# Hashed attention and channel mix on one core: pairs 2 and 3 prepared by the joint q-and-k path, with a new hand-off order for all engines

## The chip, the cores and the metric

The kernel runs on one core of a Trainium2 chip. A core has five engines that each work through their own list of instructions in order: TensorE (PE in the profile, its weight loads PEld), VectorE (DVE), ScalarE (ACT), GpSimd (POOL) and SyncE (SP, which here only starts DMA transfers). They wait for one another through semaphores. The metric is the device time of one execution in microseconds; lower is better.

## What is computed

Inputs are q, k and v of shape (4, 8, 768, 64), a projection of 64 by 6, and the weights of a channel mix. For each of the 32 (batch, head) pairs the reference computes

```python
q_bucket = np.sum(((q @ proj) > 0) * powers, axis=-1)      # six sign bits per row
k_bucket = np.sum(((k @ proj) > 0) * powers, axis=-1)
scores = np.where(q_bucket[..., :, None] == k_bucket[..., None, :], (q @ k.T) / 8, -1e9)
attn = softmax(scores)                                      # over the keys
x = (attn @ v)                                              # heads put side by side: (4, 768, 512)
xk = mu_k * x + (1 - mu_k) * x_prev                         # x_prev: one row earlier
xr = mu_r * x + (1 - mu_r) * x_prev
out = sigmoid(xr @ w_r) * (relu(xk @ w_k) ** 2 @ w_v)
```

The output is (4, 768, 512) in float32.

## The kernel before

**Pairs.** The work on attention is cut into 16 pairs n = 0 to 15. A pair is two heads of one batch (j = 0, 1), and four pairs make up a batch. After the fourth pair of a batch its channel mix (`add_moe`) can run.

**The steps of a pair.** For pair n the names are these. `ldq` (L330) brings q and k of both heads into `nat`, `ldv` (L335) brings v into `vn`. `hi` (L398, DVE) rounds q and k to float16 into the first 64 columns of `nh`, and `lo` (L401, DVE) writes the rounding remainder into the other 64. `tr` (L405, SP) is a DMA that transposes `nh` into `a`, where the rows are the head dimension and the columns the sequence. `bits` (L427, PE) projects `a` to the hash bits; `bx` (L431, DVE) turns the signs into +-64 values; four `row` copies (L443, POOL), one for each of q0, q1, k0 and k1, put them into six rows of `a`, so that one matmul gives the score and the bucket comparison together. `sc` (L544, PE) makes nine tiles of scores (`scn_0` to `scn_8`, 1024 columns each), `exp` (L548, ACT) turns each into probabilities. `oo` (L566 and L571, PE) multiplies with v, `rc` and `ob` (DVE) divide by the row sum, `ot` (PE) or `otd` (SP, a transposing DMA) transposes the result, and `xt`, `xs`, `df`, `xk`, `xr` (DVE) mix it with the row before. `vsum` (L356 to L362, POOL) and `mean` (PE) prepare v.

**Three ways of preparing.** Pairs 0 and 1 (`FIRSTS`) are transposed on PE without any DMA (`add_prep_turn`: `y`, `x`, `t` on PE at L478, L489 and L512, `ey` and `ev` on ACT or DVE, `ex` on DVE at L497). All other pairs go through `add_prep`. A pair that isn't in `MERGED` runs `hi`, `lo` and `tr` twice, once for q and once for k, each over half of the buffers; a pair in `MERGED` runs each once over the whole buffer. In both cases q and k of a pair lie in the two halves of the same buffers, `nat` (three of them), `nh` (two) and `a` (four).

```python
whole = n in MERGED
for side in ("qk",) if whole else "qk":
    nat, nh, a = (nat_t[s], nh_t[sh], a_t[sa]) if whole else (side_nat[side][s], ...)
```

**Channel mix.** `kp` (L659, PE), `relu` (ACT), `sq` (DVE), `r` (L679, PE), `tanh` (ACT), `v` (L692, PE), `os` (L699, DVE) and `st` (L702, SP: the store). Its weights come in by `wl` (SP) and are cast by `wc` (POOL).

**The order.** The functions only describe operations, in program order. The list `ORDER` (L17) gives the sequence in which all of them are issued, as indices into that program order; it was computed ahead of time and is written out. Because every engine works in order, `ORDER` fixes each engine's own sequence. `BANKS` (L72) gives each PSUM tile, in program order, its place: 0 to 3 for a 4 KB score tile, 0 to 7 for a half of one. A tile can be written only after the last reader of the tile that had the place before. `warm` and `warmb` (L246, L251) are matmuls on zeros that keep PE occupied; `warm` is 14 of them, each of the eight `warmb` is two. `table` (L253, ACT) makes ACT load its function table.

Of the kernel before, what the change touches and what calls it, by code (L numbers as in the profile page):

```python
# [128 lines left out]
def kernel(  # L129
# [34 lines left out]
    MERGED = tuple(range(4, 16))  # L164
# [225 lines left out]
    def add_prep(n):  # L390
        s, sh, sa = n % NQ, n % NNH, n % NAQ
        whole = n in MERGED
        for side in ("qk",) if whole else "qk":
# [385 lines left out]
```

## Time and profile before

| What | Value |
|---|---|
| three runs | 243.22, 243.06, 242.08 us; median 243.06 us |
| the profiled execution | 242.0 us, of which the span from first to last instruction is 240.2 us |
| granted TensorE clock, mean | 1.00 |
| busy of the span | PE 97%, DVE 75%, ACT 76%, POOL 41% |
| DMA queue q1 | 43.20 MB, 70.9% of the 16 DMA engines' span |

Busy counts the time in which at least one instruction of the engine runs. The profiled execution takes 1.8 us more than its span; that lies before the first and after the last instruction. A figure such as "x12" in a row is a count of instructions, and "idle before" names what the engine waited for.

### The profile page before, as it was taken

To read this page: it belongs to the slowest core of one execution; us is meant where nothing else is said; L and a number is where in the kernel's file an instruction comes from. 1 tells how busy PE (TensorE), PEld (TensorE's weight loads), DVE (VectorE), ACT (ScalarE), POOL (GpSimd) and SP (SyncE) were. 2 spreads that over 40 slices of the span, in tenths; PEclk is the share of its full clock that TensorE was granted. 3 is DMA by queue.
4 is the path that set the end of the run, shared out by engine and by line. 5 is a ranking of instruction groups with operands and counts; after the bars stand their busy time and mean duration, and the time that the engine had idled before them with its cause. 6 is when DMAs were issued, how large, how long until landed. Compare 5 with 4: busy or idle time off the path is not lost.

```text
span 240.2 us, 6251 instructions
## 1 busy us (share of the span) xinstructions
PE 234.1 (97%) x2515; PEld 147.8 (62%) x2532; DVE 179.8 (75%) x388; ACT 181.9 (76%) x242; POOL 99.7 (41%) x148
## 2 busy tenths in 40 slices
PE   8999999999999999999999999999999999999994
PEld 6985776776766565656456656665566564455442
DVE  3488789999998898989868896887167867348232
ACT  2699999999999999889779999677884640256320
POOL 4064979989934899438087302550000000000000
PEclk9999999999999999999999999999999999999999
DMA  6989999999999999988999989401500401210333
GB/s 225 304 222 274 232 242 260 279 197 362 279 253 284 273 213 294 249 302 206 276 163 241 249 177 234 136 0 26 173 0 3 120 3 44 87 46 1 131 135 131
DMA packets 72605, 44.00 MB, mean 183 GB/s; under 512 B 54912, under 2 KB 67584, under 8 KB 72576
## 3 DMA queue, kind: packets, MB, share of 16 engines
q1 hardware_dynamic: 72208, 43.20, 70.9%
q8 instruction: 20, 0.33, 0.6%
q10 hardware_dynamic: 368, 0.39, 0.5%
q14 instruction: 9, 0.07, 0.1%
HBM read 24.12 MB, written 6.29 MB: 127 GB/s over the span
## 4 chain that ended last, share of the span: by engine, by line
PE 92%; ACT 5%; issue 1%; DVE 0%
PE ps_all L544 25%; PE ps_all L692 17%; PE ps_all L659 16%; PE ps_all L571 14%; PE ps_all L679 8%; ACT pt L548 4%; PE ps_all L427 4%; PE ps_all L489 2%; PE ps_all L512 1%; PE ps_all L478 1%; ACT kr L663 1%; PE ps_all L251 1%; PE ps_all L246 1%; PE ps_all L599 1%; PE ps_all L566 1%
## 5 line engine op out<-in xcount | busy, mean ns | idle before, releaser
L548 ACT ACTIVATE pt<-ps_all 128x1024 bf16<-128x1024 f32 x144 | 138.4, 1041 | 10.9 <-PE ps_all L544 10.3
L544 PE MATMUL ps_all<-a 128*128 128x256 f16 (+1 forms) x384 | 79.2, 325 | 0.5 <-ACT pt L548 0.3
L443 POOL COPY a<-bx 6x384 f32<-6x384 f32 x56 | 38.9, 695 | 34.4 <-DVE bx L431 19.6
L544 PEld LDWEIGHTS <-a 128*128 128x128 f16 x384 | 34.0, 98 | 23.5 <-issue 4.6
L659 PE MATMUL ps_all<-xk,wk 128*128 128x384 bf16 x256 | 48.3, 326 | 0.1
L571 PEld LDWEIGHTS <-pt 128*128 128x128 bf16 x1152 | 42.5, 97 | 8.0 <-issue 0.5
L692 PE MATMUL ps_all<-wv,k 128*128 128x512 bf16 (+2 forms) x199 | 45.6, 362 | 0.5
L571 PE MATMUL ps_all<-va,pt 128*128 128x65 bf16 x1152 | 44.8, 193 | 0.0
L663 ACT ACTIVATE kr<-ps_all 128x384 bf16<-128x384 f32 x64 | 29.4, 491 | 16.0 <-PE ps_all L659 14.4
L659 PEld LDWEIGHTS <-wk 128*128 128x128 bf16 x256 | 24.2, 98 | 17.0 <-issue 0.6
L692 PEld LDWEIGHTS <-k 128*128 128x128 bf16 x208 | 19.3, 98 | 18.9 <-issue 0.3
L699 DVE SCALAR_TENSOR_TENSOR os<-rs,ps_all 128x512 f32<-128x512 f32 (+2 forms) x26 | 16.5, 643 | 19.0 <-PE ps_all L692 13.7
L682 ACT ACTIVATE rs<-ps_all 128x512 f32<-128x512 f32 x24 | 14.3, 602 | 20.5 <-PE ps_all L679 14.1
L666 DVE TENSOR_TENSOR k<-kr 128x384 bf16<-128x384 bf16 x64 | 23.2, 389 | 8.3 <-ACT kr L663 8.3
L401 DVE SCALAR_TENSOR_TENSOR nh<-nat,nh 128x1536 f16<-128x1536 f32 (+1 forms) x16 | 27.0, 1694 | 0.2
L679 PE MATMUL ps_all<-wr,xr 128*128 128x512 bf16 x88 | 23.2, 379 | 0.4
L356 POOL TENSOR_TENSOR vt<-vn 128x384 f32<-128x384 f32 x12 | 17.8, 1485 | 12.5 <-DMA vn<-in_v_dram 11.7
L589 DVE TENSOR_TENSOR ob<-ps_all,rc 128x384 bf16<-128x384 f32 x32 | 17.5, 553 | 1.4 <-DMA xt<-ob 0.8
L431 DVE TENSOR_SCALAR bx<-ps_all 128x768 uint16<-128x768 uint16 x14 | 13.4, 956 | 5.3 <-PE ps_all L427 4.7
L398 DVE TENSOR_SCALAR nh<-nat 128x1536 f16<-128x1536 f32 (+1 forms) x16 | 15.8, 985 | 0.3 <-PE ps_all L512 0.2
L679 PEld LDWEIGHTS <-xr 128*128 128x128 bf16 x96 | 9.0, 98 | 9.0
L380 DVE SCALAR_TENSOR_TENSOR va<-ps_all,vn 128x384 bf16<-128x384 f32 x24 | 12.7, 548 | 0.5 <-PE ps_all L375 0.2
(77 smaller groups left out, 188.9 us busy)
## 6 DMA issues: line engine op xcount, KB each, us to landing
vn<-in_v_dram SPq DMA_DIRECT2D x16, 384.0 KB, 5.1
out_dram<-os SPq DMA_DIRECT2D x23, 256.0 KB, 2.3
nat<-in_k_dram SPq DMA_DIRECT2D x15, 384.0 KB, 4.7
nat<-in_q_dram SPq DMA_DIRECT2D x15, 384.0 KB, 5.2
wst<-in_moe_w_k_dram SPq DMA_DIRECT2D x2, 512.0 KB, 7.0
wst<-in_moe_w_r_dram SPq DMA_DIRECT2D x2, 512.0 KB, 5.8
wst<-in_moe_w_v_dram SPq DMA_DIRECT2D x2, 512.0 KB, 4.4
k<-in_moe_w_k_dram SPq DMA_DIRECT2D x1, 512.0 KB, 4.4
```

Of the source, the lines that this page charges most:

```text
L356: e.tensor_tensor(out=vt[:, :, :, 0:E], in0=src[:, :, 0:3, 0:E], in1=src[:, :, 3:6, 0:E], op=ALU.add)
L401: nc.vector.scalar_tensor_tensor(out=nh[:, :, D:P], in0=nat.rearrange("p j (c d) -> p (j c) d", d=D), scalar=QS, in1=nh[:, :, 0:D], op0=AL ...
L443: nc.gpsimd.tensor_copy(side_a[side][n % NAQ][D : D + NB, j, :].bitcast(FP32), bx_t[sx][32 * i : 32 * i + NB, :].bitcast(FP32))
L544: nc.tensor.matmul(ps[:, lo - s * STEP : hi - s * STEP], side_a["k"][sa][:, j, jc * P : (jc + 1) * P], side_a["q"][sa][:, j, q0 : q0 + hi ...
L548: nc.scalar.activation(out=pt_t[sp][:, s * STEP : (s + 1) * STEP], in_=ps_t[plan.slot[nm]], func=AF.Exp, bias=EBIAS, scale=ESC)
L571: nc.tensor.matmul(oo[:, ic * 65 : ic * 65 + 65], pt_t[sp][:, o : o + P], va_t[sa][:, j, jc, 0 : D + 1], start=(not uc and ic == 0 and jc ...
L589: nc.vector.tensor_tensor(out=ob_t[so][:, :, j * D : (j + 1) * D], in0=oo[:, :, 0:D], in1=rc_t[sr][:, 1, :].unsqueeze(2).to_broadcast([P, ...
L659: nc.tensor.matmul(ps[:, 0:HALF], wk_sb[:, d, fc * P : (fc + 1) * P], xk_t[mx[d]][:, h * HALF : (h + 1) * HALF], start=(d == 0), stop=(d = ...
L663: nc.scalar.activation(out=kr_t[sk], in_=sm(nm)[:, 0:HALF], func=AF.Relu, scale=0.5 ** 0.5)
L666: nc.vector.tensor_tensor(out=k2_t[s2][:, h * HALF : (h + 1) * HALF], in0=kr_t[sk], in1=kr_t[sk], op=ALU.mult)
L679: nc.tensor.matmul(sm(nr), xr_t[mx[d]][:, c * P : (c + 1) * P], wr_sb[:, d, :], start=(d == 0), stop=(d == NDC - 1))
L692: nc.tensor.matmul(sm(nv)[:, x0:x1], k2_t[(b * NFC + fc) % NK2][:, c * P : (c + 1) * P], wv_sb[:, fc, x0:x1], start=(fc == 0), stop=(fc == ...
```

## The change

`MERGED` now begins at 2 instead of 4. Pairs 2 and 3 thereby have one `hi`, one `lo` and one `tr` each instead of two, six operations fewer in all (1326 instead of 1332), and the indices in `ORDER` shift. `ORDER` and `BANKS` are replaced throughout.

```diff
 ORDER = [
-    0, 16, 2, 3, 4, 21, 5, 6, 7, 20, 8, 9, 10, 11, 37, 41, 33, 26, 1, 29, 28, 36, 30, 32, 40, 69, 72, 71, 70, 74, 73, 25, 43, 27, 31, 79,
+    69, 0, 2, 3, 4, 5, 6, 7, 8, 9, 10, 11, 12, 16, 31, 13, 14, 15, 84, 72, 1, 39, 42, 71, 74, 25, 32, 70, 24, 33, 73, 77, 75, 76, 90, 78,
...
 BANKS = [
-    2, 6, 2, 0, 4, 0, 0, 0, 0, 4, 4, 0, 3, 7, 1, 5, 4, 6, 1, 4, 5, 3, 4, 5, 2, 3, 4, 5, 4, 3, 0, 1, 2, 3, 0, 0, 0, 1, 7, 6, 6, 0, 2, 2, 2,
+    4, 2, 7, 3, 3, 2, 3, 7, 4, 3, 0, 0, 2, 4, 7, 1, 6, 6, 5, 2, 1, 1, 4, 7, 4, 2, 0, 1, 0, 3, 2, 2, 0, 1, 0, 1, 1, 3, 0, 1, 1, 3, 2, 1, 0,
...
-    MERGED = tuple(range(4, 16))
+    MERGED = tuple(range(2, 16))
```

Read as names, engine by engine, the beginnings of the two orders are these (a digit after a name is the pair, "1k" is q or k of pair 1; `oo0_0` stands three times in the list because it is issued in three parts):

```
SP before  0q0 0q1 pw1 1k 2k mur 2q 3k 1q v0 v1 3q tr2 tr2 4k v2 4q muk v3 tr3 tr3 5q 5k tr4 6q 6k v4 tr5 wl2 v5 wl0 wl1 tr6
SP after   0q0 0q1 pw1 1k v0 1q v1 2q 2k v2 4k 3q 3k tr2 4q v3 v4 muk tr3 5q 5k mur 6k 6q tr4 v5 v6 tr5 wl0 wl1 tr6
ACT before 0k0 0k1 pw0 ey0k0 ey0q0 ey0q1 ey0k1 table evt0k0 ey1k0 evt0k1 exp0_1 ...
ACT after  0k0 0k1 table pw0 ey0q0 ey0k0 ey0k1 ey0q1 evt0k0 ey1k0 evt0k1 exp0_1 ey1q0 ...
PE before  [14 warm, warmb 0 5 4 3] y0k0 y0q0 y0q1 y0k1 x0k0 x0q0 t0k0 warmb1 t0q0 x0k1 y1k0 t0k1 x0q1 sc0_1 ...
           t1q1 sc0_5 t1q0 sc1_8 sc1_6 sc1_3 bits2 sc1_7 sc1_4 sc1_5 oo0_1 oo0_1 oo0_0 oo0_0 sc1_0 oo0_0 sc2_3
PE after   [14 warm, warmb 0] y0q0 y0k0 y0q1 y0k1 warmb5 x0k0 warmb3 x0k1 x0q0 t0k0 t0k1 y1k0 t0q0 warmb4 x0q1 sc0_1 ...
           t1q0 sc0_5 t1q1 sc1_3 warmb2 sc1_6 sc1_8 sc1_5 bits2 oo0_0 sc1_7 sc1_4 oo0_0 sc1_0 oo0_0 sc1_1 oo0_1 oo0_1 oo0_1 sc2_2
DVE before ... evt0q1 hi2 lo2 lo2 ex1k0 ... hi3 hi3 lo3 bx2 lo3 hi4 lo4 rc0 rc0 ob0 ob0
DVE after  ... evt0q1 hi2 lo2 ex1k0 evt1k0 hi1q0 evt1k1 ex1q0 evt1q0 evt1q1 hi3 lo3 bx2 rc0 ob0 [muk + (-1)] hi4 lo4
POOL rows  pair 2 before: k0 q0 k1 q1, after: k0 q1 k1 q0; pair 3 before: q1 k1 q0 k0, after: q0 k1 q1 k0
```

115 rows, old and new, of tables (BANKS, ORDER) are left out of this document.

## The prediction

> **What bounds the kernel now.** I read the page first: busy shares and the chain of work that ended last.
>
> ```profile
> PE 234.1 (97%) x2515; PEld 147.8 (62%) x2532; DVE 179.8 (75%) x388; ACT 181.9 (76%) x242; POOL 99.7 (41%) x148
> PE 92%; ACT 5%; issue 1%; DVE 0%
> ```
>
> PE is busy for 234.1 us, 97% of the span, and makes 92% of the chain. Next I cut the span into stretches, to see where the rest of its 240.2 us lies. The columns are the stretch, its length, then busy time of PE, PEld, DVE, ACT and POOL.
>
> ```profile
> 0.00:5.20 5.20, 4.01 (x22) 2.99 (x23) 1.49 (x4) 1.28 (x1) 2.42 (x22) 1.00 0.63 203
> 5.20:21.50 16.30, 16.30 (x157) 13.56 (x155) 11.29 (x26) 13.59 (x19) 7.08 (x13) 1.00 0.94 266
> 21.50:39.60 18.10, 18.08 (x285) 12.55 (x284) 15.77 (x25) 18.10 (x21) 13.82 (x17) 1.00 1.08 255
> 39.60:60.00 20.40, 20.39 (x315) 14.01 (x315) 19.89 (x38) 20.19 (x23) 18.73 (x21) 1.00 1.11 273
> 60.00:90.00 30.00, 29.56 (x379) 19.49 (x378) 27.96 (x57) 29.51 (x41) 21.27 (x25) 1.00 1.12 261
> 90.00:230.00 140.00, 139.10 (x1322) 81.56 (x1337) 100.46 (x237) 98.01 (x139) 36.32 (x53) 1.00 0.53 136
> 230.00:240.20 10.20, 6.68 (x44) 3.61 (x42) 2.97 (x6) 1.19 (x2) 0.00 (x0) 0.99 0.42 155
> ```
>
> PE's idle time is 1.19 us at the start, 3.52 us in the last stretch, and 0 + 0.02 + 0.01 + 0.44 + 0.90 = 1.37 us in the 224.8 us between. The change leaves PE's instructions as they are: it has no matmul more or less. So **before has almost nothing to give back**: all PE waits together are worth 1.37 us, 0.6% of the time, and whatever PE newly waits for is added to the end, since no later idle time absorbs it. From 21.5 to 90 us ACT is as full (18.10 of 18.10, 20.19 of 20.40, 29.51 of 30.00), and the DMA share (column before the last) is about 1: in that stretch a late operand has little cover. That is where pairs 2 and 3 stand.
>
> **The change part by part.** Six operations go. What they cost is in these rows: durations are min/median/max in ns, then the first and the last start; the row behind each transfer is its time from issue to landing. First come all 16 transposes, then those of pair 2 (two halves), pair 3 (two halves), pair 4 and pair 14.
>
> ```profile
> L398 DVE TENSOR_SCALAR nh<-nat x16: 548/1034/1264, 11.3 to 140.2; 128x1536 f16<-128x1536 f32 x12, 128x768 f16<-128x768 f32 x4
> L401 DVE SCALAR_TENSOR_TENSOR nh<-nat,nh x16: 948/1756/2427, 13.1 to 141.8; 128x1536 f16<-128x1536 f32 x12, 128x768 f16<-128x768 f32 x4
> L405 SPq DMA_TRANSPOSE a<-nh x16: 1381/4284/5971, 14.1 to 145.1; - x16
> DMA to landing us min/median/max: 3.9/6.9/9.5
> ...
> L405 SPq DMA_TRANSPOSE a<-nh x2: 1381/1649/1917, 14.1 to 15.5; - x2
> DMA to landing us min/median/max: 3.9/4.0/4.2
> ...
> L405 SPq DMA_TRANSPOSE a<-nh x2: 1946/2084/2223, 22.3 to 24.3; - x2
> DMA to landing us min/median/max: 5.0/5.5/6.0
> ...
> L405 SPq DMA_TRANSPOSE a<-nh x1: 5022/5022/5022, 28.2 to 28.2; - x1
> DMA to landing us min/median/max: 8.4/8.4/8.4
> ...
> L405 SPq DMA_TRANSPOSE a<-nh x1: 3579/3579/3579, 140.3 to 140.3; - x1
> DMA to landing us min/median/max: 7.0/7.0/7.0
> ```
>
> On DVE a pair's two halves take 2 x 0.55 + 2 x 0.95 = 3.0 us and the joint form 1.03 + 1.76 = 2.8 us: 0.2 us per pair, on an engine that is not the bound. On the DMA the joint form is no gain in time to landing. Of pair 3's halves the second lands 5.0 us after its issue; joint ones take 8.4 us behind loads (28.2) and 7.0 us behind a queue that is nearly empty (140.3). Since all of `lo` must be done before a joint one starts, its data come **2 us later** after `lo` (7.0 against 5.0). [...]
>
> The rest is the new order, which I follow as PE's lateness against before. The rows for the start, from the order of time and, last, of the `pw` transfers (L326):
>
> ```profile
> 1.59 0.85 PE L246 MATMUL ps_all<-k 128*128 128x256 bf16 x3
> 2.23 0.63 PE L251 MATMUL ps_all<-k 128*128 128x256 bf16 x2
> ...
> 1.67 0.56 ACTq L326 DMA_DIRECT2D pw<-in_proj_dram  x1
> 2.26 1.28 ACT L483 ACT_TABLE_LOAD   x1 [2.26 <-issue]
> 4.77 0.38 PE L251 MATMUL ps_all<-k 128*128 128x256 bf16 x2
> 4.99 0.38 PE L246 MATMUL ps_all<-k 128*128 128x256 bf16 x2
> 5.21 1.47 PE L478 MATMUL ps_all<-pt,nat 128*128 128x128 f32 x12
> 6.51 1.41 PE L489 MATMUL ps_all<-pw,pt 128*128 128x12 f32 x12
> 7.23 0.22 ACT L253 ACTIVATE tb<-tb 128x1 f32<-128x1 f32 x1
> DMA to landing us min/median/max: 3.5/3.6/3.7
> ```
>
> 1. **Fillers.** 16 instead of 22 zero matmuls stand ahead of the first `y`, so `y` can start at about 4.6 instead of 5.2: 16 x 0.213 (three take 0.64, from 1.59 to 2.23) after the first at 1.19. What was taken away comes later: six of the eight `warmb` stand ahead of `bits2` instead of five (+0.22 us, from 4.77 to 4.99 for two matmuls), and 13 score tiles instead of 12 (+0.43 us, 1024 columns). With no wait at all PE would reach `bits2` at 21.53 (row below) + 0.65 = 22.2.
> 2. **`pw`.** ACT issues `pw` after `table` now, so 1.28 + 0.22 = 1.5 us later, at 3.2. Landing takes 3.6 us: 6.8. PE has done four `y` (0.33 each, from 5.21 to 6.51 for four) and a filler at about 6.1 and stands before `x0k0`: 0.7 us, or nothing if the transfer is that much faster. I take 0.4.
> 3. **`ex1k0`** stands behind the joint `hi2` and `lo2`. The order of the loads has 2k sixth. The first lands at 2.3 + 4.8 = 7.1 and the others follow at 393 KB / 374 GB/s = 1.05 us (row below): 2k at 12.3. From `x0k0` at 6.5, PE needs 6.2 us to the end of `t0q1`, and DVE's copy after it ends at 13.4; `lo2` ends at 16.2 and `ex1k0` at 16.4, when PE comes to `t1k0` (16.7). Waits between 0 and 0.3, I take 0.1, and as much for single waits for a PSUM place.
>
> So PE is at `bits2` at 22.2 + 0.6 = 22.8 (22.2 to 23.4).
>
> ```profile
> nat<-in_k_dram SPq DMA_DIRECT2D x15, 384.0 KB, 4.7
> GB/s 374 384 353 364 277 173 299 354 389 231 118 148 154 276 323 358 369 358 384 394 399 369 333 343 374 410 399 405 404 306 62 20 5 0 84 219 212 207 221 178
> L330 SPq DMA_DIRECT2D nat<-in_k_dram x2: 471/524/577, 2.3 to 2.9; - x2
> DMA to landing us min/median/max: 4.8/4.8/5.2
> 21.53 0.83 PE L427 MATMUL ps_all<-a,p 128*32 128x512 f16 x16
> 31.39 0.83 PE L427 MATMUL ps_all<-a,p 128*32 128x512 f16 x16
> 39.64 0.83 PE L427 MATMUL ps_all<-a,p 128*32 128x512 f16 x16
> 22.49 0.96 DVE L431 TENSOR_SCALAR bx<-ps_all 128x768 uint16<-128x768 uint16 x1 [0.24 <-PE ps_all L427]
> L443 POOL COPY a<-bx x4: 503/1108/1922, 23.6 to 27.9; 6x384 f32<-6x384 f32 x4
> ```
>
> 4. **`tr2`** is issued at 16.3 and lands at 16.3 + 7.0 = 23.3 (5.6 by the two halves of pair 2, 8.4 by pair 4: 21.9 to 24.7). `bits2` waits 0.5 (0 to 1.9). It starts at 23.3: 1.1 us late for the work done by then.
> 5. **The rows of pair 2.** `bx2` now stands behind a whole `lo3`, which ends 24.6 (`t1q1` ends 1.95 us of work ahead of `bits2`, at 20.9, `evt1q1` at 21.6, then 1.1 + 1.9), so it ends at 25.6. The first score tile, `sc2_2`, needs q0 and k0, and q0 is the fourth row instead of the second. Four rows take 4.8 us beside `hi` and `lo` (0.50 to 1.92 each), and 2.2 us where DVE leaves them alone. Here DVE waits for `oo0_0` meanwhile, so I take the short form: done at 27.9. PE has 4.2 us of other work after `bits2` (24.1), four score tiles and six parts of `oo`: 28.3. Wait 0.1 with the spread of the rows (0 to 2.2).
> 6. **`tr3`.** Issued after `lo3`, 24.7 + 7.0 = 31.7 (30.2 to 33.1). PE comes to `bits3` at 31.39 + 1.2 = 32.6. No wait (0 to 0.5).
> 7. **`tr4`** isn't merged anew, but it is moved behind four loads and one 2 KB transfer (5q, 5k, mur, 6k, 6q; before only 5q and 5k), and all of them behind `tr3`, whose issue holds SP for 4.3 (the median) to 5.0 us. SP is free at 29.4, the five issues take 2.4 us, so `tr4` goes out at 31.8 instead of 28.2 and lands after 7.0 to 8.4 us, at 38.8 to 40.2. `bits4` stands 0.3 us of work earlier in PE's order than before: 39.64 - 0.3 + 1.2 = 40.5. No wait (0 to 0.4).
>
> Sum until `bits4`: 0.6 + 0.5 + 0.1 + 0 + 0 = **1.2 us late**. All later transposes are at about their old place with more slack, by the lists of names; the totals of work on each engine ahead of the later `bits`, `sc` and `exp` agree within about 0.5 us until pair 14. For other new waits between 40 and 100 us, where ACT and PE are both full, I take 0.2 (from -0.8, when before's own waits there vanish, to 0.6). The tail ends with the same three pieces of the last tile: 0.
>
> So 240.2 + 1.4 = 241.6 us of span, 243.4 us for the execution beside the profiled 242.0. That execution lies 1.06 us under the median of 243.06, so on the scale of the medians I predict **244.4 us**, 0.6% slower.
>
> **The rivals.**
>
> *Absorbed: no slower than before (the other side).* The mechanism is in steps 2 and 4: if `pw` lands at 6.1 (2.9 us after issue instead of 3.6) and `tr2` within 6.4 us of its issue, `x0k0` and `bits2` start without wait, and PE is at `bits2` at 22.2 to 22.4; steps 5 to 7 then leave 0.2 to 0.4. For it: pair 2's two halves together took 5.6 us (issued at 14.1 and 15.5, 4.2 to land). Against it: the joint ones quoted take 7.0 and 8.4 us, and the median of all is 6.9. Time 243.1 - 0.3 to 243.1 + 0.8, so 242.8 to 243.9. [...] The case decides where `pw` is 0.7 and `tr2` 0.6 us faster than I take them.
>
> *Before's own waits vanish.* The most that can be had is the 1.37 us between 5.2 and 230: 241.7. It needs every wait of before to go and none to come, and steps 2 to 4 name three that can come; I give it a tenth.
>
> *The rows collide.* In step 5 the rows meet `hi4` and `lo4` and take 4.8 us: `sc2_2` at 30.5 instead of 28.3, 2.2 us on PE and on ACT, which has no other tile left. Together with the 1.1 us of the steps before and the same for pair 3, where the third row is needed instead of the second (one row more, 1.1): 243.1 + 1.1 + 2.2 + 1.1 = 247.5. For it: before's rows of pair 2 took 4.8 us. Against it: DVE's order has `rc0` and `ob0` between.
>
> *The merge does nothing by itself*, and the order is all. That is part of each case.
>
> **How the numbers follow.** Forecast 0.41 (243.7 to 245.4, three quarters of it over the bound), absorbed 0.27, waits vanish 0.10, rows collide or another stall of more than 2.3 us 0.22. A measurement of this kernel can tell about 0.5% (1.2 us) from no change. Slower by more: 0.41 x 0.75 + 0.22 = 0.53; within: 0.10 + 0.27 = 0.37; faster by more: 0.10. The range leaves out the vanished waits and the far end of the collision: 242.3 to 247.5.
>
> **What would show it.** PE's idle time in 5.2 to 21.5 (forecast about 0.6, at `x0k0` above all, beside none before), then a `bits2` at 23 us that waits for `a<-nh`, `bits4` near 40.4, and `sc2_2` at about 28 with a wait for POOL L443. After 60 us PE should be as full as before. I would be wrong if PE shows no idle time to 40 us, if a wait of several us stands after 60 us, or if the first rows take 1.1 us and more each.

## The result and the profile after

The changed kernel takes **253.47 us** (median of 6 runs, 251.22 to 254.43), before 243.14 us (6 runs): ratio 1.043, 95% interval 1.040 to 1.046. The direction of the forecast was right, its size was not: 10 us instead of 1.4. The profiled execution takes 252.63 us, its span is 250.7 us, 10.5 us longer than before's. Four executions below (two of e6, one each of e9 and e11) took clearly longer than the others of their kernel and are left out of its ratio and of its time.

First the page of the changed kernel: the busy shares, then the chain by engine and the head of its list by line.

```profile
PE 238.6 (95%) x2515; PEld 152.6 (61%) x2532; DVE 181.6 (72%) x384; ACT 181.6 (72%) x242; POOL 100.4 (40%) x148
...
PE 77%; DMA 8%; ACT 7%; DVE 5%; issue 2%; SPq 0%; DVEq 0%; ACTq 0%
PE ps_all L543 18%; PE ps_all L658 17%; PE ps_all L691 16%; PE ps_all L570 10%; PE ps_all L678 8%; ACT pt L547 7%; DMA a<-nh 4%; DMA pw<-in_proj_dram 4%; PE ps_all L426 3%; PE ps_all L488 3%; PE ps_all L511 2%; DVE xk L634 1%; DVE df L629 1%; DVE nh L400 1%; PE ps_all L477 1%
```

PE fell from 92% of the chain to 77%, and a DMA that wasn't there before, `pw`, has 4%. (Lines of the changed kernel are one less than before: `x` is L488, `bits` L426, `pw` L325.) The same stretches as before, in the same columns, with the granted clock of TensorE third from the end:

```profile
0.00:5.20 5.20, 4.01 (x19) 3.08 (x20) 0.80 (x3) 1.49 (x2) 1.38 (x13) 1.00 0.66 198
5.20:21.50 16.30, 11.63 (x80) 10.97 (x79) 3.75 (x11) 4.91 (x8) 8.54 (x23) 0.69 0.55 193
21.50:39.60 18.10, 18.03 (x224) 12.88 (x222) 13.76 (x19) 17.59 (x21) 4.63 (x9) 1.00 0.94 202
39.60:60.00 20.40, 19.32 (x299) 13.13 (x297) 19.34 (x32) 19.74 (x22) 16.16 (x20) 1.00 1.17 228
60.00:90.00 30.00, 29.56 (x384) 20.09 (x381) 29.46 (x61) 28.91 (x40) 21.11 (x24) 1.00 1.12 293
```

Nearly all of it is in one row, 5.2 to 21.5 us: PE works 11.63 us instead of 16.30, and its clock there (1.00 is full speed) is 0.69 instead of 1.00. What happens in that row, from the order of time:

```profile
1.67 1.28 ACT L252 ACT_TABLE_LOAD   x1 [1.67 <-PEq L762]
...
2.96 0.20 ACT L252 ACTIVATE tb<-tb 128x1 f32<-128x1 f32 x1
...
4.42 1.02 SPq L329 DMA_DIRECT2D nat<-in_q_dram  x1
4.57 2.14 PE L477 MATMUL ps_all<-pt,nat 128*128 128x128 f32 x12
...
5.19 0.60 ACTq L325 DMA_DIRECT2D pw<-in_proj_dram  x1
...
11.60 1.43 PE L488 MATMUL ps_all<-pw,pt 128*128 128x12 f32 x6 [4.67 <-DMA pw<-in_proj_dram]
```

`y` starts at 4.57 and `table` ends at 3.16, as forecast. But `pw` goes out at 5.19 instead of 3.2, and PE then stands for **4.67 us** before `x0k0`. The rows of `pw` (SP's half, then ACT's), who waited for it, and the time to landing:

```profile
L325 SPq DMA_DIRECT2D pw<-in_proj_dram x1: 562/562/562, 1.7 to 1.7; - x1
L325 ACTq DMA_DIRECT2D pw<-in_proj_dram x1: 602/602/602, 5.2 to 5.2; - x1
...
  PE ps_all L488: 4.7, 1
...
DMA to landing us min/median/max: 3.5/4.9/6.3
```

SP's half lands after 3.5 us, at 5.17, and ACT's is issued right then, at 5.19. The trace's records of the two issues show that they have one semaphore in common (106), and ACT's waits for it: SP's half counts on it from 4.70 to 5.17. In before the halves have two (107 and 106), neither waits, and ACT's goes out at 1.67. Here it then takes 6.3 us, to 11.47. The second load of q ahead of it (issued at 4.42) lands after 7.2 us, at 11.6:

```profile
L329 SPq DMA_DIRECT2D nat<-in_q_dram x1: 1023/1023/1023, 4.4 to 4.4; - x1
...
DMA to landing us min/median/max: 7.2/7.2/7.2
```

So 1.5 KB (64 x 6 float32) arrive together with the last of five 384 KB loads that SP had issued earlier. The trace's record of DMA packets shows that the data themselves are late: the 64 pieces of 24 bytes of ACT's half move between 9.15 and 10.74 us, 4.0 us and more after the issue; in before, between 4.08 and 4.94, 2.4 us and more after it.

The second loss is the clock; stretches of the changed kernel, columns as above:

```profile
8.00:9.20 1.20, 0.00 (x0) 0.00 (x0) 0.00 (x0) 0.00 (x0) 0.67 (x1) 1.00 1.05 390
9.20:9.40 0.20, 0.00 (x0) 0.00 (x0) 0.00 (x0) 0.00 (x0) 0.20 (x4) 0.86 1.09 393
9.40:11.60 2.20, 0.00 (x0) 0.03 (x1) 0.00 (x0) 0.00 (x0) 2.04 (x10) 0.50 1.06 385
11.60:15.60 4.00, 4.00 (x20) 3.94 (x21) 0.66 (x3) 0.00 (x0) 3.77 (x9) 0.50 0.13 45
15.60:19.20 3.60, 3.60 (x28) 3.48 (x28) 0.79 (x3) 1.56 (x3) 1.86 (x5) 0.50 0.00 0
19.20:19.60 0.40, 0.40 (x5) 0.40 (x3) 0.40 (x1) 0.40 (x2) 0.00 (x0) 0.52 0.20 42
19.60:31.30 11.70, 11.67 (x104) 8.95 (x104) 7.67 (x14) 10.57 (x13) 0.00 (x0) 1.00 0.77 193
```

The clock falls to half during the idle time, at 9.34 (0.86 in the row from 9.20), and comes back at 19.58: 10.24 us. PE is fully "busy" from 11.60 on, but six matmuls of `x` take 1.43 us (the row at 11.60), where before twelve took 1.41. Of the 10.24 us PE works in 7.98, which by this estimate costs half of it, 4.0 us. **4.67 + 4.0 = 8.7 of the 10.5 us**; 1.8 us are left for all other steps, against 1.0 in the forecast (1.4 less 0.4 for `pw`).

### The profile page after: what moved, and what is told of

It is laid out like the page before. It is cut to its first block, busy times and chain, and to the rows that moved or that the text cites. A ratio compares the mean times of both kernels' runs of the same rounds, so it can differ in the third digit from the quotient of the medians.

```text
span 250.7 us, 6244 instructions
## 1 busy us (share of the span) xinstructions
PE 238.6 (95%) x2515; PEld 152.6 (61%) x2532; DVE 181.6 (72%) x384; ACT 181.6 (72%) x242; POOL 100.4 (40%) x148
## 4 chain that ended last, share of the span: by engine, by line
PE 77%; DMA 8%; ACT 7%; DVE 5%; issue 2%; SPq 0%; DVEq 0%; ACTq 0%
PE ps_all L543 18%; PE ps_all L658 17%; PE ps_all L691 16%; PE ps_all L570 10%; PE ps_all L678 8%; ACT pt L547 7%; DMA a<-nh 4%; DMA pw<-in_proj_dram 4%; PE ps_all L426 3%; PE ps_all L488 3%; PE ps_all L511 2%; DVE xk L634 1%; DVE df L629 1%; DVE nh L400 1%; PE ps_all L477 1%
## 5 line engine op out<-in xcount | busy, mean ns | idle before, releaser
L570 PEld LDWEIGHTS <-pt 128*128 128x128 bf16 x1152 | 43.3, 97 | 8.4 <-DVE va L379 0.6
L570 PE MATMUL ps_all<-va,pt 128*128 128x65 bf16 x1152 | 45.5, 193 | 0.4 <-DVE va L379 0.4
L665 DVE TENSOR_TENSOR k<-kr 128x384 bf16<-128x384 bf16 x64 | 23.9, 394 | 11.6 <-ACT kr L662 11.5
L400 DVE SCALAR_TENSOR_TENSOR nh<-nat,nh 128x1536 f16<-128x1536 f32 x14 | 26.2, 1869 | 0.2
L355 POOL TENSOR_TENSOR vt<-vn 128x384 f32<-128x384 f32 x12 | 19.9, 1660 | 5.6 <-DMA vn<-in_v_dram 4.8
L397 DVE TENSOR_SCALAR nh<-nat 128x1536 f16<-128x1536 f32 x14 | 14.6, 1045 | 0.0
```

Of the source, the lines that this page charges most:

```text
L355: e.tensor_tensor(out=vt[:, :, :, 0:E], in0=src[:, :, 0:3, 0:E], in1=src[:, :, 3:6, 0:E], op=ALU.add)
L400: nc.vector.scalar_tensor_tensor(out=nh[:, :, D:P], in0=nat.rearrange("p j (c d) -> p (j c) d", d=D), scalar=QS, in1=nh[:, :, 0:D], op0=AL ...
L570: nc.tensor.matmul(oo[:, ic * 65 : ic * 65 + 65], pt_t[sp][:, o : o + P], va_t[sa][:, j, jc, 0 : D + 1], start=(not uc and ic == 0 and jc ...
L665: nc.vector.tensor_tensor(out=k2_t[s2][:, h * HALF : (h + 1) * HALF], in0=kr_t[sk], in1=kr_t[sk], op=ALU.mult)
```

## The experiments

Theory A: the late `pw`, with the clock that falls behind it, makes the loss, and the rest of the change costs 1 to 2 us. Rivals: the merge or the new order as a whole makes it. Kernels named together ran beside the same runs of before, whose median is given.

**e1 to e4** (before: 242.43 us).

e1_pw_first takes the new kernel and undoes one hand-off:

```python
order.remove(at["table"])
order.insert(order.index(at["ldpw0"]) + 1, at["table"])
```

> The changed kernel with one operation moved: ACT issues its transfer of proj (pw) before it loads its function table, as the kernel before does; the merge, the loads, the places and all other orders stay. Theory A (the late pw alone makes the loss: 4.7 us of PE idle before L488 and then about 10 us at half the granted clock): x0k0 starts at about 6.2, bits2 at about 22.5 instead of 31.7, clock 1.00, and the time is 0.5 to 1.5 us over the kernel before, 243.6 to 244.6. Rival B (the order of the loads, with v0, 1q and v1 ahead of 2q and 2k, or the merge, delays the start): bits2 stays near 30 and the time within 2 us of the changed kernel, over 251.

Measured 244.5 us, ratio 1.009 (1.006 to 1.012), span 242.2: one instruction moved gives back 8.5 of 10.5 us of span. `pw` is issued at 1.68, the clock is 1.00 from 6.9 to 15.6 us, and three waits of PE stay until 50 us (`x` and the following lines are four higher here; `ex1k0` is L500, `ob` L592):

```profile
16.81 0.51 PE L515 MATMUL ps_all<-idh,nh 128*128 128x128 f16 x6 [0.47 <-DVE nh L500]
32.37 0.51 PE L602 MATMUL ps_all<-idb,ob 128*128 128x128 bf16 x6 [0.26 <-DVE ob L592]
41.73 0.83 PE L430 MATMUL ps_all<-a,p 128*32 128x512 f16 x16 [0.82 <-DMA a<-nh]
```

e2_table_first does the opposite: before, with that one hand-off of the change.

```python
order.remove(at["table"])
order.insert(order.index(at["ldpw0"]), at["table"])
```

> The kernel before with one operation moved: ACT loads its function table before it issues pw, as the changed kernel does. Theory A: pw goes out after the table at 3.2 or, since its semaphore is that of q of pair 0 here, at 3.8, and lands behind the transfers issued before it, 1k and 2k, at about 8.1, as in the changed kernel it landed with 2q at 11.5. PE idles about 1.6 us before x0k0, too short for the clock to fall (in the changed kernel it fell 2.1 us after PE went idle), so 1.5 to 2.5 us over the kernel before: 244.6 to 245.6. Rival: a transfer on ACT's queue does not stand behind those of SP's, pw lands 3.7 us after issue at the latest (7.5), and the time is 0 to 1 us over the kernel before. Rival B: no more than 0.5 us over it.

The expectation was missed: 250.21 us, ratio 1.031 (1.027 to 1.034). No merge and no other new order is in it, and yet it loses 7.8 us, flat from `bits2` to the end. `pw` goes out at 3.94 and lands at 9.71, with 2q again (issued 4.12, landed 9.89). I had the landing at 8.1, by the two large loads ahead of it, and a full clock; it came 1.6 us later, with a load that SP issued 0.18 us behind it. The stretches:

```profile
7.00:9.80 2.80, 0.00 (x1) 0.03 (x1) 0.00 (x0) 0.70 (x2) 0.01 (x1) 1.00 0.97 293
9.80:12.00 2.20, 2.19 (x26) 2.12 (x27) 0.70 (x4) 0.33 (x1) 0.84 (x4) 1.00 0.96 314
12.00:22.20 10.20, 10.20 (x52) 7.97 (x50) 6.12 (x10) 5.49 (x7) 6.68 (x9) 0.50 0.25 87
22.20:29.60 7.40, 7.40 (x71) 5.94 (x70) 4.40 (x11) 6.54 (x8) 0.12 (x1) 1.00 1.04 254
```

Idle time is only 2.80 us, and the clock falls 2.2 us after PE has begun to work again; 10.2 us at half cost 5.1 by the same estimate. 2.8 + 5.1 = 7.9 of its 8.4 us of span. By the starts, `x0k0` is 3.3 us later than before and `bits2` 8.1, so 4.8 us are lost between them.

e3_bridge is the new kernel with one filler made longer, so that PE isn't idle while it waits for `pw`:

```python
for _ in range(42 if i == 5 else 2):
```

> The changed kernel with 40 more matmuls on zeros just before x0k0, where PE sits idle for 4.7 us; they take 40 x 0.107 = 4.3 us, so x0k0 still starts at 11.6, but PE does not go idle. Theory A: the granted clock stays at 1.00, the 7.6 us of work from 11.6 to 19.2 take 3.8 us, and the time is 3.3 to 4.0 us under the changed kernel, about 249.7. Rival: what runs in these 7.6 us is bound by the transfers and by ACT, and the clock costs nothing: within 0.5 us of the changed kernel.

Measured 249.8 us, ratio 1.032 (1.028 to 1.035), clock 1.00 from 5.2 to 19.3 us: 3.0 us of span less than the new kernel, though `x0k0` starts no earlier than 11.28. From there to `bits2` it takes 16.4 us, the new kernel 20.1: so the half clock cost 3.7 us, nearly the estimate of 4.0. `bits2` and `bits3` come 4.0 us earlier than in the new kernel; of that 0.6 us goes into a longer wait for a transpose at `bits4` (0.9 us in the new kernel), and the rest is lost later:

```profile
46.44 0.83 PE L426 MATMUL ps_all<-a,p 128*32 128x512 f16 x16 [1.55 <-DMA a<-nh]
```

e4_merge_only is before with pairs 2 and 3 merged, the joint operation at the place of the later half, and nothing else:

```python
MERGED = tuple(range(2, 16))
```

> The kernel before with pairs 2 and 3 merged (one hi, lo and tr each, at the place of the later half), all other orders and all places as before. Theory A: the joint tr2 goes out at 15.0 and lands at about 22, 0.5 us after PE wants it, the joint tr3 at 24.4 and lands at about 31.4, when PE wants it: 0.3 to 1.0 us over the kernel before, 243.4 to 244.1. Rival B (the merge itself is what costs): over 3 us slower. The other side (one transfer is cheaper than two): equal or up to 0.5 us faster.

Missed: 245.14 us, ratio 1.010 (1.008 to 1.013), 2.7 us instead of 0.3 to 1.0. The joint `tr2` and `tr3` land 5.5 and 6.0 us after issue; what is late are rows, `ob` and a transpose of a later pair:

```profile
29.76 0.38 PE L549 MATMUL ps_all<-a 128*128 128x512 f16 x1 [0.28 <-POOL a L448]
48.27 0.51 PE L604 MATMUL ps_all<-idb,ob 128*128 128x128 bf16 x6 [0.48 <-DVE ob L594]
89.22 1.47 PE L549 MATMUL ps_all<-a 128*128 128x256 f16 x8 [0.16 <-POOL a L448]
94.79 0.83 PE L432 MATMUL ps_all<-a,p 128*32 128x512 f16 x16 [0.75 <-DMA a<-nh]
```

So the merge does cost something by itself in before's order, 1%, and it is no rival for 10 us. These four waits are 1.7 of the 3.4 us by which its profiled span is longer; the rest isn't traced here.

**e5, e6, e7, e9** (before: 242.80 us).

e5_pw_on_sp leaves `table` where the change put it and issues both halves of `pw` on SP (`nc.sync.dma_start(out=pw[...`).

> The kernel after, table still ahead on ACT, but both pw transfers are issued on SP, one behind the other and ahead of the large loads. Theory A, that only pw's place between the transfers counts: pw is issued at about 2.3, lands within 3.5 to 3.7 us (before: 3.5 to 3.7) at about 5.9, PE goes from y to x0k0 with under 0.3 us of idle time, the granted clock stays at 1.0, and the time is that of e1_pw_first, 244.5 (244.0 to 245.2; the SP loads go out 0.6 us later). Rival B, that an early table costs by itself or that the loads moved by 0.6 us cost as much as pw did: over 246.

On `pw` theory A holds: landing takes 3.2 to 3.6 us, nobody waits for it, the mean clock is 0.999, and `bits2` is 1.65 us later than before (e1: 1.72). The time misses the range: 245.9 us, ratio 1.013 (1.007 to 1.018). The rest comes 35 us later, from the rows of pair 5 on POOL. The same two waits, 1.06 and 0.18 us, stand in e11 below, where `pw` goes out on ACT as in e1, so the place of `pw` isn't needed for them; why they come here and not in e1 isn't shown:

```profile
56.75 0.38 PE L543 MATMUL ps_all<-a 128*128 128x512 f16 x1 [1.06 <-POOL a L442]
57.31 0.38 PE L543 MATMUL ps_all<-a 128*128 128x512 f16 x1 [0.18 <-POOL a L442]
```

e6_pw_split is e1_pw_first with pairs 2 and 3 as halves again, both at the joint operation's place (`MERGED = tuple(range(4, 16))`).

> e1_pw_first with pairs 2 and 3 as two halves each again (both halves at the places of the joint one). Theory A, that the merge costs what e4_merge_only showed (245.14 against 242.43): the 2 us that e1_pw_first is over before go, 242.4 to 243.4. Rival B, that the new order costs them: 244.2 to 245. If both share it, about 243.8.

Measured 243.9 us, ratio 1.005 (1.003 to 1.007) against e1's 1.009 (1.006 to 1.012). Theory A (the merge costs all of it) is missed: some 1.1 us stay without the merge, about half of what is left, and belong to the order (243.8 was the value for both sharing it). Whether the merge costs the other half here isn't settled, since the intervals overlap. It waits for `ex1k0` (0.59 us) and `ob` (0.51) as e1 does, and no more for `tr4`.

e7_table_bridge is e2_table_first with `range(22 if i == 3 else 2)` in the filler.

> e2_table_first with 22 zero matmuls instead of 2 in the filler ahead of the last two warm ones, 20 x 0.107 = 2.1 us more, which delay the first y to about 7.3 and leave about 0.8 us of the 2.9 us of idle time ahead of x0k0. Theory A, that half of the loss of e2_table_first is the granted clock that falls after an idle time: no row at half clock, PE at bits2 about 3 us later than before instead of 8, time 245.3 (244.8 to 246.0). Rival B, that the clock falls whenever the first x is late, or for the loads: still 10.24 us at half clock, about 250.

Measured 245.95 us, ratio 1.012 (1.008 to 1.016), where e2 had 1.031. The clock is 1.00 from 5.2 to 25.3 us, although `pw` lands as late (5.5 us after issue) and `x0k0` starts at 9.47:

```profile
4.74 2.57 PE L255 MATMUL ps_all<-k 128*128 128x256 bf16 x22
...
9.47 1.48 PE L493 MATMUL ps_all<-pw,pt 128*128 128x12 f32 x12 [0.63 <-ACT pt L487]
```

So the idle time drops the clock, and not the late `x` or the loads (the 0.63 us that are left of it don't): 20 useless matmuls of 2.1 us save 4.6 us of span (248.6 to 244.0).

e9_small_ahead is the new kernel with two 2 KB transfers in the places of two 384 KB loads ahead of `pw`:

```python
old = ("ldv0", "ldv1", "ldv2")
new = ("mur", "muk", "ldv0")     # ldv1 and ldv2 go behind ldq4k
```

> The kernel after, with the 2 KB transfers mur and muk in the places of the 384 KB loads of v of pairs 0 and 1, v of pair 0 in the place of v of pair 2, and v of pairs 1 and 2 behind 4k; pw waits for the same landing as in the kernel after. Theory A, that the small transfer lands no earlier than the loads issued ahead of it on SP: pw is issued at 5.2 as before it, but with three large loads ahead instead of five it lands 2 x 1.04 = 2.1 us earlier, at 9.4, just ahead of 2q, and PE idles 2.6 us ahead of x0k0 instead of 4.7. The clock should still fall for 10.24 us, as after the 2.9 us of e2_table_first, so the time is about 251.4 (250.5 to 253, the late v of pair 1 may add). Rival B, that the landing takes 6 us by itself after a wait on a landing: pw lands at 11.5 again, idle time 4.7, 253.5.

Measured 251.2 us, ratio 1.035 (1.030 to 1.039). The time is as expected by luck: the idle time is 4.1 us instead of 2.6, and the half clock lasts 6.8 us instead of 10.24. The landing at 10.6 lies between the two theories. The reason is in the issues of SP: 2k goes out at 5.00 now, just ahead of `pw` at 5.12, so four loads are ahead of it and not three. Three would have been 9.4, one more is 1.04: 10.4. It lands again with the last of them (`pw` after 5.5 us at 10.61, 2k after 5.8 at 10.77). The clock:

```profile
6.60:10.70 4.10, 0.02 (x1) 0.00 (x0) 0.26 (x1) 0.74 (x2) 0.00 (x0) 1.00 0.95 318
10.70:11.20 0.50, 0.46 (x5) 0.49 (x5) 0.00 (x0) 0.00 (x0) 0.00 (x0) 0.97 0.14 52
11.20:18.00 6.80, 6.80 (x44) 6.61 (x44) 2.29 (x6) 1.62 (x3) 3.55 (x11) 0.50 0.00 0
18.00:30.50 12.50, 12.21 (x107) 9.20 (x106) 8.87 (x14) 11.22 (x13) 6.80 (x12) 1.00 0.91 241
```

**e8, e10, e11** (before: 242.64 us).

e10_tr4_early is e1_pw_first with `tr4` ahead of `mur` in the order.

> e1_pw_first with tr4 issued ahead of the loads mur, 6k and 6q instead of behind them (about 1.5 us earlier on SP). Theory A, that step 7 of the forecast was under-sized (0, where e1_pw_first shows 0.99 us of waiting for a<-nh at 40.5 us): that wait goes, bits4 starts 0.7 to 1.0 us earlier and the time is 243.6 (243.2 to 244.0). Rival B, that the transposes wait for one another or for a free buffer, and not for the issues ahead: the wait stays or moves to the next transposes, 244.5.

Measured 244.04 us, ratio 1.006 (1.003 to 1.009): the wait at `bits4` is gone, as theory A has it, and one for the next transpose is there, as rival B has it; the time lies between the two:

```profile
49.52 0.83 PE L432 MATMUL ps_all<-a,p 128*32 128x512 f16 x16 [0.98 <-DMA a<-nh]
```

In e1 `tr4` lands 9.9 us after its issue behind five transfers. Here it lands after 6.2 us, and `tr5`, which now has five transfers ahead of it, after 11.2. So in these two runs the landing goes with the transfers ahead, which speaks for theory A's reason, but the delay was handed on and not saved.

e11_tr4_no_fill and e8_no_late_fill leave out the matmuls of four late fillers, in e10 and in before:

```python
for _ in range(0 if i in (1, 2, 6, 7) else 2):
```

> e10_tr4_early without the zero matmuls of the four fillers warmb1, warmb2, warmb6 and warmb7 (8 matmuls of 0.107 us, after PE has its first real work; nothing of the result depends on them). If PE is the bound there, 0.86 us less than e10_tr4_early at most: 242.8; if the operands behind them set the pace, the same time.

> The kernel before without the zero matmuls of the fillers warmb1, warmb2, warmb6 and warmb7. PE is at 97% there with no idle time between 5.2 and 60 us, so they should cost their own 0.86 us: 0.4 to 0.9 us less than before. If the work behind them waits for operands instead, no change.

Neither is faster: 244.4 us (ratio 1.006, 1.002 to 1.010) and 243.34 us (1.003, 1.000 to 1.005). In e8, where before had none, PE now waits for a row:

```profile
96.21 1.46 PE L544 MATMUL ps_all<-a 128*128 128x512 f16 x8 [0.68 <-POOL a L443]
```

So leaving out 0.86 us of zero matmuls gained nothing that can be measured, though PE shows 97%. No version beat before.

## Why the prediction was wrong

The step that failed is **step 2, `pw`**: "Landing takes 3.6 us: 6.8", and of the wait "I take 0.4" (bounds 0 to 0.7). It measured 4.67 us of waiting and 4.0 us of lost clock, as e1 shows from the one side and e2 from the other. Three things were wrong in it.

- The issue. I had it follow `table` at 3.2; it waits for another transfer's landing until 5.19. That is 2.0 us. The wait stands in the trace's record of the issue (semaphore 106, last count at 5.17), not in the kernel's source.
- The landing. 3.6 us was `pw` with only pair 0's four loads ahead of it; 6.3, 6.0, 5.8, 5.5 and 5.5 us are what it takes behind loads (after, e3, e2, e9, e7). The forecast's own price for loads was near, if `pw` had been put into the row with them: 2.3 + 4.8 = 7.1 for the first, and 1.05 us for each further one. Five loads give 11.3, measured 11.47 (after) and 11.15 (e3); four give 10.3, measured 10.61 (e9). With two it is a lower bound: 8.2, measured 9.71 (e2) and 9.38 (e7). Even for an issue at 3.2, with two loads out, it gives a wait of 2.1 us instead of 0.4. The 24-byte pieces of data moved late too (from 9.15 us on in after, 4.0 us after the issue). Why they waited isn't shown.
- The clock. The stretches of before show no granted clock under 0.99, so a wait was priced at its own length. After 2.8 to 4.7 us of idle time the half clock cost another 3.4 to 5.1 us by the estimate (3.7 measured by e3 for after's 4.0). In after the clock fell 2.4 us into the idle time; in e2 2.80 us of it were enough. PE was busy at half clock for 6.8 us in e9, 7.98 us in after and 10.2 us in e2 before the clock was full again. What sets these lengths isn't shown.

The other steps are tested by e1, in which `pw` is as before. **Step 1** had the start of `y` right, 4.57 (4.6), but not its pace. The fillers ahead of it take 0.21 us each at first and 0.11 later, in before too: the first matmul starts at 1.19 in both, and the clock is full at 4.52 in before's profiled execution, ahead of `y`, and at 5.93 in after's, where `y` takes 2.14 us instead of 1.47 and PE stands before `x0k0` at 6.93 instead of 6.1. In e1 it is 5.15 and `y` takes 1.76. (In the thirteen profiled executions this moment lies between 3.92 and 6.55, so by half of that difference, up to 1.3 us, PE can be later in one profile than in another for this alone; that is an estimate.) **Step 3** was short: `t1k0` waits 0.47 us for `ex1k0` (0.1, bounds 0 to 0.3). **Step 4** was long: `tr2` lands at 22.2, 5.5 us after issue, and `bits2` (23.25) doesn't wait (0.5, bounds 0 to 1.9). **Step 5**: no wait for pair 2's rows (0.1), but 0.26 us for `ob`, which I hadn't named. **Step 6** was right: `bits3` doesn't wait. **Step 7** had the issue exact (31.8) and the landing short: 9.9 us instead of 7.0 to 8.4, so `bits4` waits 0.82 us (0, bounds 0 to 0.4). The sum is 2.0 us of span where the terms without `pw` gave 1.0, and on the medians 2.1; the three waits and the 0.3 us of `y` are 1.85 of it. So the other steps, each off by up to 0.8 us and in both directions, missed by 1 us; step 2 missed by 8.3 (4.67 + 4.0 - 0.4). That the direction was right doesn't speak for the mechanism: the forecast's slowdown came from small waits, and the measured one from a term that it had put at 0.4.

Of the rivals none was it: "another stall of more than 2.3 us" had the size, without the place. "The merge does nothing by itself" is refuted by e4 for before's order.

That before had "almost nothing to give back" holds for what is added. For what is taken away PE's 97% misled: e8 took 0.86 us of PE's work away and gained nothing (1.000 to 1.005).

## What to carry to other kernels

A small transfer wasn't small here when it went out behind large ones (1.5 KB on ACT landed after 6.3 us in after and 3.7 in before): price its landing from the loads issued ahead of it, SP's too (within 0.4 us for four or five loads here, 1.2 to 1.6 us too early for two), and look in the trace for what its issue waits for. An idle time of PE cost 1.8 to 2.8 times its length here (4.67 us and 4.0 us of lost clock in after, 4.1 and 3.4 in e9, 2.8 and 5.1 in e2, the lost clock by the estimate): 2.8 to 4.7 us of it halved the clock for 7 to 10 us, and single ones of up to 1.55 us (e3) did not; cheap matmuls that only bridge it saved 3.0 and 4.6 us of span. When such an input is late, move its one issue forward before touching anything else: here that was worth 8.5 us.

## What was not expected of the hardware

- The clock fell after 2.80 us without a matmul, and 2.2 us after the work had begun again (e2). In the profiled executions it stayed at half for 6.8 or 10.2 us, all but the first 2.3 us of it (in after) under full load. The six executions of the changed kernel have mean clocks of 0.973, 0.980 and 0.986, two each; if only this stretch lowers it, that is some 14, 10 and 7 us at half (an estimate from the mean and the span).
- ACT's transfer of 1.5 KB landed within 0.2 us of a 384 KB load of SP: the last one issued before it in after and e9, and one issued just 0.17 to 0.18 us after it in e2 and e7. In e3 it landed 0.6 us ahead of the last one before it.
- In e1 and e10 `tr2`, `tr3` and the moved `tr4` land after 5.5 to 6.6 us, `tr5` of e1 behind two loads after 9.1, and the two that stand behind five transfers (four of them loads) after 9.9 and 11.2 us; moving one forward made the next one slow.
